# The router's small tables: from SBUF into a corner of the accumulator's PSUM bank

## Chip, cores and metric

One NeuronCore of a Trainium2 chip runs the whole program. The metric is the device time of one execution in microseconds (us). The profiled execution is one more run of the same program with the hardware profiler on.

## What is computed

Causal attention with a decaying bias, and behind it a layer of eight experts with one expert per token.

```
scores = q @ k.T / 8 ; bias = -(cum[i] - cum[j]),  cum = cumsum(max(s, 0))
attn   = softmax(where(causal, -1e9, scores + min(bias, 0)))      # 8 batches, 8 heads, 576 x 576
x      = (attn @ v) laid out as 4608 tokens x 512
logits = (x / |x|) @ (emb / |emb|).T / tau                        # 8 experts
e      = argmax(logits) ; gate = softmax(logits)[e]
out    = gate * (relu(x @ w1[e]) @ w2[e])                         # w1: 512 x 1024, w2: 1024 x 512
```

## The kernel before

The order of the work is written out by hand (`manual_schedule`): each engine runs its instructions in the order in which the Python code issues them, and the framework adds the semaphore waits that the data needs. For PSUM it orders any two accesses of different engines to the same bank, whether or not their columns overlap.

**Attention, 64 steps.** `step(n)` works on head `n`. In one step TensorE (PE) computes the scores of head `n` (`ta_`, `tb_`, `tbm`, `tbl`), a first pass of scores for head `n+5` from which VectorE (DVE) takes the row maxima (`s1`, `sa`, `s3`, `sb`; matmuls on L361, maxima on L369, L406 and L409), and at its end the product of probabilities and values of head `n-2` (`pv`, L525 to L527). Those products accumulate in columns 0 to 364 of one PSUM bank, the tile `om`. The score tiles `s` of the first pass have two buffers, so PE cannot start the third of a step before DVE has taken the maxima of an earlier one. ScalarE (ACT) does the exponentials (L497, L500) and casts. GpSimd (POOL) forms the low half of each probability, `PL = P - high half`, a subtraction with both inputs in SBUF (`pl_`, L251), 1024 and 576 columns per step, and issues the loads of q and k (L258, L338) and the scatters of finished tokens (L669). At the start of the next step DVE turns `om` into a finished head of tokens (`norm1` to `norm3`: L538, L542, L550). The heads of a batch are eight steps in a row.

**The router.** When the last head of batch `b` is normalised, `router(b, xt)` queues a chain of small DVE operations in `tasks`, and `slots` takes a few of them at the end of each step, up to the next `None`:

- first step: `sume` sums the logits (L79, 40 numbers per partition) and `sel1` takes their maxima (L607);
- second step: `sel2` marks the candidates (L611), `sel3` weighs them (L614);
- third step: `sel4` picks one (L618), `sel5` makes the one-hot table `oh` of it (L622);
- fourth step: PE ranks the tokens of each expert by ten small matmuls into columns 368 to 415 of `om` (`rank0`, L629 to L635), and at the end of that step DVE adds the base (L638, L640), selects (L646) and reduces to the target rows (L650).

The first batch's chain starts in step 10, and every eighth step after that. For batches 0 to 5 (`nb` is 8) it falls into the regular stretch of attention; batch 6 falls into the last steps, where the slots lie elsewhere, and batch 7 behind the loop. The scratch of the chain lies in SBUF, in slices of the tile `idx`: `IX["L"]` (40 columns: logits), `IX["T"]` (40: candidates, later ranks) and `IX["w"]` (5: maxima of the candidates). The columns of `IX["L"]` also serve once, in step 10, as a block of zeros that eight DMAs on the SP queue copy to the token table (`zr` in `setup4`, L241 and L242).

**The experts.** Behind step 63 the tokens are gathered by expert and run through both weight matrices (L891 and L967), the weights streaming in through a ring of buffers.

Of the kernel before, what the change touches and what calls it, by code (L numbers as in the profile page):

```python
# [76 lines left out]
def esum(nc, L, x):  # L77
    e = x.rearrange("p j (q a e) -> p j e q a", q=4, e=NE)[:, :, :, :, ::17]
    nc.vector.tensor_reduce(L, e, AX.XY, ALU.add)  # L79
# [35 lines left out]
def main(ctx, tc, qkh, qkc, vtin, s_in, emb, tau, w1h, w2h, out, shared, nb):  # L115
# [7 lines left out]
    ps_m, om = shared["ps_m"], shared["om"]  # L123
# [95 lines left out]
    IX = {}  # L219

    def setup4():
# [7 lines left out]
        nc.gpsimd.tensor_copy(IX["gp"], IX["tmp"].bitcast(I32))  # L229
        IX["L"], IX["T"], IX["w"] = t[:, 284:324], t[:, 324:364], t[:, 364:369]  # L230
        IX["r"], IX["E"] = t[:, 224:244], t[:, 244:284]
# [366 lines left out]
    def router(b, xt):  # L598
        R = {}

        def sume():
            R["L"] = IX["L"].rearrange("p (j e) -> p j e", j=5)
            esum(nc, R["L"], xt[:, :, 0:XW])

        def sel1():
# [1 line left out]
            nc.vector.tensor_reduce(m[:, 0], R["L"], AX.X, ALU.max)  # L607

        def sel2():
            T = R["T"] = IX["T"].rearrange("p (j e) -> p j e", j=5)  # L610
            nc.vector.tensor_tensor(T, R["L"], R["m"][:, 0].unsqueeze(2).to_broadcast([128, 5, NE]), op=ALU.is_ge)  # L611

        def sel3():
            nc.vector.tensor_tensor(R["T"], R["T"], wval, op=ALU.mult)  # L614

        def sel4():
            R["w"] = IX["w"]
            nc.vector.tensor_reduce(R["w"], R["T"], AX.X, ALU.max)  # L618

        def sel5():  # L620
# [16 lines left out]
        def rank1():  # L637
            nc.vector.tensor_tensor(R["T"], R["pr"][:, 0:40].rearrange("p (j e) -> p j e", j=5),  # L638
                                    base.unsqueeze(1).to_broadcast([128, 5, NE]), op=ALU.add)
            nc.vector.tensor_add(base, base, R["pr"][:, 40:40 + NE])  # L640
            if nb - 4 < b < nb - 1:
                nc.vector.tensor_copy(IX["cnt0"][:, 0:1], base[:, 0:1])
                nc.vector.tensor_scalar(base[:, 0:1], base[:, 0:1], float(SPL if b == nb - 3 else SPM), None, op0=ALU.max)

        def rank2():
            nc.vector.tensor_tensor(R["T"], R["T"], R["oh"], op=ALU.mult)  # L646

# [36 lines left out]

        sc = [P(scat, j) for j in range(5)]
        tasks.extend([sume, sel1, None, sel2, sel3, None, sel4, sel5, P(mq.append, rank)])

    X, WT, HT = {}, {}, {}
# [1010 lines left out]
```

## Time and profile before

| | |
|---|---|
| median of 3 runs | 828.55 us (827.26 to 832.63) |
| profiled execution | 827.8 us, of which 826.1 us span |
| PE busy | 769.1 us, 93% of the span |
| DVE, ACT, POOL busy | 556.5, 569.2 and 395.3 us |
| mean granted TensorE clock | 0.966 of full speed |
| regular attention (60 to 345 us) | PE busy 263.09 of 285.00 us, clock 0.96 |

PE's busy time is the time in which at least one matmul was in flight. The clock is the share of its upper level that the throttle granted. The profile names lines of the kernel (L622 is line 622), engines and tiles with buffer numbers left out.

### The profile page before, as it was taken

The page shows a single profiled execution, that of the slowest core. Times are in us where ns is not written, and L with a number is a line of the kernel's source. Part 1 is how long each engine was busy: PE and PEld are TensorE (multiplying, and loading weights), DVE is VectorE, ACT ScalarE, POOL GpSimd, SP SyncE. Part 2 cuts the span into 40 slices and gives each one's busy share as a digit, 9 for nine tenths or more (in the row PEclk, how much of TensorE's full clock was granted, in tenths as well). Part 3 has the DMA queues.
Part 4 walks back from the last instruction along what each step waited for, and adds up shares of the span by engine and source line. Part 5 has one row for each costly group of instructions (what it writes and reads, how often), then busy time and mean ns, then how long its engine had stood idle before and what let it go on. Part 6 is the DMA issues. An engine that isn't in the chain of part 4 may idle for free. (4 is left out here: it accounts for less than half of the span.)

```text
span 826.1 us, 20954 instructions
## 1 busy us (share of the span) xinstructions
PE 769.1 (93%) x7998; PEld 552.9 (67%) x7998; DVE 556.5 (67%) x1818; ACT 569.2 (69%) x1029; POOL 395.3 (48%) x375
## 2 busy tenths in 40 slices
PE   8998898989989898999789998989989989999997
PEld 4798897989989897988454554545444544554554
DVE  7787788787878888898557765654555556645621
ACT  9898688897969897887467865827637649376410
POOL 9997596887869796873432121220221112202001
PEclk9999899999989999999989999999999989999999
DMA  7798779595949797764534855643744746534001
GB/s 162 158 196 169 137 177 193 133 209 132 199 113 216 150 209 150 177 207 129 185 99 154 190 160 158 163 153 108 177 145 112 188 151 140 177 113 124 25 13 53
DMA packets 76002, 124.01 MB, mean 150 GB/s; under 512 B 38823, under 2 KB 39231, under 8 KB 75032
## 3 DMA queue, kind: packets, MB, share of 16 engines
q0 software_dynamic: 19632, 69.69, 36.2%
q1 hardware_dynamic: 56260, 52.84, 24.1%
q8 instruction: 71, 1.16, 0.6%
q14 instruction: 39, 0.32, 0.1%
HBM read 93.99 MB, written 21.49 MB: 140 GB/s over the span
## 5 line engine op out<-in xcount | busy, mean ns | idle before, releaser
L251 POOL TENSOR_TENSOR PL<-P 128x576 f16<-128x576 f32 (+2 forms) x128 | 205.1, 1709 | 31.9 <-ACT P L500 21.7
L891 PE MATMUL h<-xH,wt 128*128 128x512 f16 (+2 forms) x560 | 155.7, 360 | 0.8 <-DVE hq L922 0.3
L891 PEld LDWEIGHTS <-wt 128*128 128x128 f16 x960 | 86.8, 100 | 84.6 <-issue 11.9
L975 POOL DMA_INDIRECT out<-Kx,xj x39 | 44.1, 1130 | 195.2 <-DVE Kx L974 165.4
L361 PE MATMUL s<-qkb 96*128 96x288 f32 (+4 forms) x272 | 98.7, 377 | 22.4 <-DVE M L369 21.8
L525 PE MATMUL om<-vh,P 128*128 128x73 f16 x960 | 110.5, 201 | 3.0 <-DVE xt L550 2.3
L737 POOL DMA_INDIRECT Qx<-xs,idx x40 | 44.3, 1107 | 140.1 <-ACT vjunk L830 70.7
L526 PE MATMUL om<-vl,P 128*128 128x72 f16 x960 | 109.7, 199 | 0.0
L527 PE MATMUL om<-vh,PL 128*128 128x73 f16 x960 | 109.5, 200 | 0.0
L526 PEld LDWEIGHTS <-P 128*128 128x128 bf16 x960 | 96.5, 101 | 4.2 <-issue 3.6
L525 PEld LDWEIGHTS <-P 128*128 128x128 bf16 x960 | 95.7, 101 | 0.5 <-DVE xt L550 0.3
L527 PEld LDWEIGHTS <-PL 128*128 128x128 f16 x960 | 95.7, 100 | 0.0
L891 PE MATMUL h<-xL,wt 128*128 128x512 f16 (+1 forms) x264 | 94.9, 366 | 0.0
L967 PE MATMUL pxs<-wt,hq 128*128 128x512 f16 x360 | 90.3, 384 | 3.3 <-DVE wt L875 3.3
L500 ACT ACTIVATE P<-tb 128x1024 f32<-128x1024 f32 x64 | 65.1, 1018 | 24.8 <-PE tb L466 23.4
L369 DVE CUSTOM_DVE_ANT_0 junk<-s,mS 128x448 bf16<-128x448 f32 (+3 forms) x144 | 73.9, 520 | 5.3 <-PE s L361 3.2
L967 PE MATMUL pxs<-wt,hp 128*128 128x512 f16 x288 | 74.5, 387 | 0.0
L361 PEld LDWEIGHTS s<-qkb 96*128 96x128 f32 x272 | 51.9, 194 | 29.8 <-DVE M L369 27.9
L974 DVE TENSOR_SCALAR Kx<-pxs,xj,idx 128x512 f32<-128x512 f32 x39 | 31.5, 808 | 54.8 <-PE pxs L967 31.7
L967 PEld LDWEIGHTS <-hq 128*128 128x128 f16 x360 | 35.5, 99 | 46.5 <-ACT vjunk L749 3.6
L463 PE MATMUL tb<-QC,KC 128*128 128x448 f32 (+3 forms) x256 | 64.5, 310 | 0.0
L459 PE MATMUL tb<-qkb 128*128 128x448 f32 (+3 forms) x256 | 62.0, 289 | 0.0
(309 smaller groups left out, 1962.1 us busy)
## 6 DMA issues: line engine op xcount, KB each, us to landing
qkb<-qkh POOLq DMA_DIRECT2D x15, 1216.0 KB
ring<-w2h SPq DMA_DIRECT2D x44, 256.0 KB
ring<-w1h SPq DMA_DIRECT2D x36, 256.0 KB
KC<-qkh POOLq DMA_DIRECT2D x14, 576.0 KB
QC<-qkh POOLq DMA_DIRECT2D x14, 576.0 KB
vT<-vtin SPq DMA_DIRECT2D x24, 320.0 KB
rw<-w1h SPq DMA_DIRECT2D x15, 256.0 KB
rw<-w2h SPq DMA_DIRECT2D x12, 256.0 KB
```

What stands on the lines that cost most here:

```text
L251: nc.gpsimd.tensor_tensor(out, a, b_, op=ALU.subtract)
L361: nc.tensor.matmul(out, G[g]["QB"][0:96, h, 128 * i:128 * i + 128], G[g]["KB"][0:96, h, lo:hi], start=True, stop=True)
L369: nc.vector.tensor_tensor_reduce(out=jk, in0=src, in1=ms, scale=1.0, scalar=NEG, op0=ALU.add, op1=ALU.max, accum_out=MP[n // 2][:, n % 2, ...
L459: nc.tensor.matmul(out, G[g]["KB"][:, h, ks:ks + 128], G[g]["QB"][:, h, 64 + qlo:64 + qhi], start=start, stop=False)
L463: nc.tensor.matmul(out, HD[n]["KC"][:, ks:ks + 128], HD[n]["QC"][:, qlo:qhi], start=False, stop=stop)
L500: nc.scalar.activation(HD[n]["P32"][:, 576:1600], HD[n]["tb"], AF.Exp, scale=0.125)
L525: nc.tensor.matmul(out, lh, vh[:, kb], start=(kb == 0), stop=False)
L526: nc.tensor.matmul(out[:, u:u + 72], lh, vl[:, kb], start=False, stop=False)
L527: nc.tensor.matmul(out, ll, vh[:, kb], start=False, stop=(kb == j))
L737: ins = nc.gpsimd.indirect_dma_start(out=x.bitcast(I32), out_offset=None, in_=src, in_offset=bass.IndirectOffsetOnAxis(ap=X[("i", e, t)][1 ...
L891: nc.tensor.matmul(h, w[:, 128 * c:128 * c + 128], x[:, c, lo:hi], start=(c == 0 and k == 0), stop=(c == 3 and k == 2))
L967: nc.tensor.matmul(y, h, w, start=(m == 0 and k == 0), stop=(m == 7 and k == 2))
```

## The change

For batches 0 to 5 the three scratch areas of the router become columns 416 to 500 of the PSUM bank `om`: logits 416 to 455, candidates 456 to 495, maxima 496 to 500. For batches 6 and 7 they stay in `idx`. Nothing else is edited.

```diff
         def sume():
-            R["L"] = IX["L"].rearrange("p (j e) -> p j e", j=5)
+            R["L"] = (IX["L"] if b > nb - 3 else om[:, 416:456]).rearrange("p (j e) -> p j e", j=5)
             esum(nc, R["L"], xt[:, :, 0:XW])
...
-            T = R["T"] = IX["T"].rearrange("p (j e) -> p j e", j=5)
+            T = R["T"] = (IX["T"] if b > nb - 3 else om[:, 456:496]).rearrange("p (j e) -> p j e", j=5)
...
-            R["w"] = IX["w"]
+            R["w"] = IX["w"] if b > nb - 3 else om[:, 496:501]
```

No instruction is added, taken away or moved on any engine; operands and waits of DVE's instructions change. In DVE's list, at the end of the router's third step of the first batch (`vl` is the low half of the values, `rm` the row maxima of the logits, `wsel` a constant table in SBUF, `oh` the one-hot table, `z` the first operation of the next step's normalisation; names in brackets are the engines or DMA queues whose semaphores are waited for):

```order
 L310 SCALAR_TENSOR_TENSOR vl<-V,sc,vh_109 128x3x144 [waits Activation_49]
-L618 TENSOR_REDUCE idx<-idx 128x5
-L622 TENSOR_TENSOR oh<-wsel,idx 128x40 [waits DVE_49]
-L538 TENSOR_SCALAR z<-om 128x5 [waits PE_49]
+L618 TENSOR_REDUCE om<-om 128x5 [waits PE_49]
+L622 TENSOR_TENSOR oh<-wsel,om 128x40 [waits DVE_49]
+L538 TENSOR_SCALAR z<-om 128x5
 L369 ISA junk,M<-s_1623,mS 128x448 [waits PE_49]
```

L622 keeps its place; one of its two tensor inputs is now in PSUM. The wait for PE's accumulation, which stood at L538, stands two instructions earlier.

In DVE's list, at the ends of the first and of the second step of the first batch's router:

```order
 L310 SCALAR_TENSOR_TENSOR vl<-V,sc,vh_109 128x3x144 [waits Activation_49]
-L79 TENSOR_REDUCE idx<-xt 128x40 [waits DMAHW4_49,DMAHW3_49,DMAHW5_49,DMAHW2_49,DMAHW6_49,DMAHW1_49,DMAHW7_49,DMAHW0_49,Pool_49]
-L607 TENSOR_REDUCE rm<-idx 128x5 [waits DVE_49]
-L538 TENSOR_SCALAR z<-om 128x5 [waits PE_49]
+L79 TENSOR_REDUCE om<-xt 128x40 [waits PE_49]
+L607 TENSOR_REDUCE rm<-om 128x5 [waits DVE_49]
+L538 TENSOR_SCALAR z<-om 128x5
```

```order
-L611 TENSOR_TENSOR idx<-idx,rm 128x40
-L614 TENSOR_TENSOR idx<-idx,wval 128x40 [waits DVE_49,Pool_49]
-L538 TENSOR_SCALAR z<-om 128x5 [waits PE_49]
+L611 TENSOR_TENSOR om<-om,rm 128x40 [waits PE_49]
+L614 TENSOR_TENSOR om<-om,wval 128x40 [waits DVE_49,Pool_49]
+L538 TENSOR_SCALAR z<-om 128x5 [waits DVE_49]
```

At L79 the waits for the eight DMAs and for POOL go, in this batch alone (the other batches' L79 had none), and a wait for PE comes; at L611 a wait for PE comes two instructions ahead of where it stood.

## Rows read from the trace of the kernel before

**Rows 1.** The page's first part: busy us, share of the span, instructions by engine.

```profile
PE 769.1 (93%) x7998; PEld 552.9 (67%) x7998; DVE 556.5 (67%) x1818; ACT 569.2 (69%) x1029; POOL 395.3 (48%) x375
```

**Rows 2.** Waits, PE, 60 to 350 us: total us, times, longest us.

```profile
PE s L361 <- DVE M L369: 21.5, 9, 3.4
```

**Rows 3.** DVE in order of time around 137 us: start us, us, engine, line.

```profile
136.78 0.18 DVE L618 TENSOR_REDUCE idx<-idx 128x5 f32<-128x40 f32 x1
137.00 4.08 DVE L622 TENSOR_TENSOR oh<-wsel,idx 128x40 bf16<-128x40 f32 x1
141.01 0.15 DVE L538 TENSOR_SCALAR z<-om 128x5 f32<-128x5 f32 x1
```

**Rows 4.** POOL in the same stretch and the one behind it.

```profile
135.52 3.36 POOL L251 TENSOR_TENSOR PL<-P 128x576 f16<-128x576 f32 x2
...
139.12 1.90 POOL L251 TENSOR_TENSOR PL<-P 128x576 f16<-128x576 f32 x1
143.89 1.90 POOL L251 TENSOR_TENSOR PL<-P 128x1024 f16<-128x1024 f32 x1 [2.88 <-ACT P L500]
```

**Rows 5.** PE in the same stretch; in brackets the idle time before, and its releaser.

```profile
136.51 0.20 PE L527 MATMUL om<-vh,PL 128*128 128x73 f16 x1
...
141.75 0.40 PE L361 MATMUL s<-qkb 96*128 96x288 f32 x1 [3.33 <-DVE M L369]
...
146.78 0.20 PE L527 MATMUL om<-vh,PL 128*128 128x73 f16 x1
```

**Rows 6.** Single steps between ends of accumulation: length; PE, PEld, DVE, ACT, POOL; clock; DMA.

```profile
78.27:85.24 6.97, 5.07 (x73) 4.70 (x73) 4.67 (x20) 5.05 (x8) 4.73 (x4) 1.00 0.42 109
171.54:176.63 5.09, 5.07 (x73) 4.70 (x73) 4.64 (x20) 5.06 (x8) 4.03 (x4) 1.00 0.64 188
90.22:101.78 11.56, 8.24 (x83) 7.77 (x83) 8.07 (x19) 6.17 (x10) 6.17 (x5) 0.70 0.74 130
136.71:146.98 10.27, 6.94 (x83) 6.51 (x83) 8.10 (x19) 6.22 (x10) 6.20 (x5) 0.83 0.78 145
181.55:191.78 10.23, 6.89 (x84) 6.47 (x83) 8.11 (x19) 6.24 (x10) 6.21 (x5) 0.83 0.80 149
226.33:237.95 11.62, 8.26 (x83) 7.78 (x82) 8.13 (x19) 6.24 (x10) 6.23 (x5) 0.72 0.71 134
272.70:280.27 7.57, 5.39 (x83) 5.02 (x83) 6.77 (x19) 5.58 (x9) 6.64 (x5) 1.00 1.05 183
314.89:325.12 10.23, 6.91 (x83) 6.48 (x83) 8.06 (x19) 6.23 (x10) 6.20 (x5) 0.83 0.82 148
```

**Rows 7.** Single lines: times, ns min/median/max, first and last start, forms.

```profile
L622 DVE TENSOR_TENSOR oh<-wsel,idx x8: 194/4064/4104, 90.5 to 386.9; 128x40 bf16<-128x40 f32 x8
L611 DVE TENSOR_TENSOR idx<-idx,rm x8: 190/730/742, 85.2 to 385.4; 128x40 f32<-128x40 f32 x8
L550 DVE TENSOR_TENSOR xt<-om,z x64: 531/533/535, 37.5 to 381.5; 128x360 f32<-128x360 f32 x64
L310 DVE SCALAR_TENSOR_TENSOR vl<-V,sc,vh x63: 496/646/668, 31.6 to 375.9; 128x432 f16<-128x432 f32 x32, 128x288 f16<-128x288 f32 x31
L638 DVE TENSOR_TENSOR idx<-om,base x8: 189/200/201, 101.8 to 391.7; 128x40 f32<-128x40 f32 x8
L646 DVE TENSOR_TENSOR idx<-idx,oh x8: 189/192/194, 102.1 to 392.9; 128x40 f32<-128x40 f32 x8
L640 DVE TENSOR_TENSOR base<-base,om x8: 161/162/164, 102.0 to 391.9; 128x8 f32<-128x8 f32 x8
```

**Rows 8.** The SP queue in step 10.

```profile
78.73 0.22 SPq L242 DMA_DIRECT2D xs<-idx  x1
```

**Rows 9.** DVE's first router instruction in the first and in the third batch.

```profile
80.25 0.73 DVE L79 TENSOR_REDUCE idx<-xt 128x40 f32<-128x320 f32 x1 [1.84 <-POOL PL L251]
...
171.61 0.77 DVE L79 TENSOR_REDUCE idx<-xt 128x40 f32<-128x320 f32 x1
```

**Rows 10.** Eight steps of batch 4, columns as in rows 6.

```profile
257.77:299.96 42.19, 39.99 (x586) 38.92 (x586) 35.74 (x141) 37.04 (x49) 35.33 (x31) 1.00 0.85 178
```

## The prediction

> **What bounds the kernel now.** I read the page's first part first: PE is busy in 93% of the span [rows 1], so the end moves only if PE's idle time or its clock changes. Next I asked whom PE waits for in the regular attention steps. One line carries nearly all of it: 21.5 us in 9 waits, the longest 3.4 us, of the first-pass score matmul for DVE's maxima [rows 2]. Nine waits in some fifty steps are not a steady bound but accidents, so I looked for what DVE does just before one. In the third router step of batch 1, L622, an operation on 40 numbers per partition, lasts 4.08 us [rows 3]. The same instruction takes 194 ns at its shortest, its median is 4064 ns [rows 7]. Its normalisation (L538) starts only when it ends, the maxima behind that, and PE's matmul at 141.75 has then idled for 3.33 us [rows 3, 5].
>
> What holds L622? POOL subtracts in that stretch, with both inputs in SBUF, and L622 has both inputs in SBUF too. L622 ends at 141.08 by its row, and POOL's last subtraction at 141.02 [rows 3, 4]. That subtraction of 576 columns took 1.90 us, as long as the next one of 1024 columns that ran alone [rows 4], so the two engines hinder each other. L611, also with two SBUF inputs, swings between 190 and 742 ns [rows 7]. Operations that take one tensor from PSUM and one from SBUF don't swing, though they run beside POOL's subtractions in every step: L550 takes 531 to 535 ns in 64 steps, and L310, which has two sizes, never more than 668 ns [rows 7]. So the hold belongs to the pair of SBUF inputs.
>
> The price to PE is more than the idle time. A window from one end of accumulation to the next shows a whole step (the borders are ends of L527, as 136.71 and 146.98) [rows 5]. The six steps with a held L622 last 11.56, 10.27, 10.23, 11.62, 7.57 and 10.23 us. [...] In batch 4 the hold was shorter, PE idled 2.18 us, and the clock stayed at 1.00 [rows 6]. [...]
>
> **The change part by part.**
>
> *The hold of L622.* In the changed kernel one of its inputs is in PSUM for batches 0 to 5. Its price then is that of its shortest run, 0.19 us, in place of 4.08. What would a step without the hold last? Batch 4 tells: 7.57 less 2.18 idle is 5.39 us, at full clock, with the ten ranking matmuls in it, and PE busy 5.39 [rows 6]. Six steps together now last 61.48 us; six of 5.39 are 32.34. The difference is **29.1 us**. By kind: six idle times (3.32, 3.33, 3.34, 3.36, 2.18, 3.32) make 18.9 us, and 10.3 us are lost clock.
>
> *The wait at L79 in batch 0.* It starts at 80.25 us after 1.84 us of idle time. The profile names POOL, but the order shows waits for eight DMAs as well, and the last of these is issued by SP at 78.73 [rows 8, 9]; it copies zeros out of the columns that L79 overwrites. With the logits in PSUM this wait is gone. PE idled for 1.90 us in that step, which was 6.97 us long with PE busy for 5.07; the same step of batch 2 took 5.09 [rows 6]. That is **1.9 us**. POOL's constants, which L614 still needs, are wanted one step later; I cost them at nothing: POOL works them off ahead of the subtractions of the same step, and PE needs those.
>
> *The hold of L611.* It falls from 0.73 to about 0.2 us in six steps, 3 us of DVE time. DVE's slack hides it: of the 21.5 us in nine waits [rows 2], the six held steps take 18.9 and batch 0's L79 takes 1.90 (above), which leaves 0.75 us in two waits for everything else. So 0, and 0.75 us for the low end.
>
> *PSUM in place of SBUF for seven small operations a batch.* The nearest rows with PSUM and SBUF inputs at the same size are L638 and L646: median 200 and 192 ns, the 8 ns times 42 instructions is 0.3 us, off the path in most places: 0. No row shows DVE writing PSUM. Its bound from above: if each of the six writing instructions of a batch cost a whole further short operation (0.2 us), 36 times that is 7 us of DVE time, of which DVE's slack takes most; from below, nothing speaks for a gain. I take 0.
> [...]
>
> *The new waits for PE.* L79, L611 and L618 now wait for PE's accumulation, which before was waited for at L538. Queued behind them on DVE is the next step's normalisation, and it waited for the same matmuls. L618 started at 136.78, and PE's accumulation had ended at 136.71; L79 of batch 2 at 171.61, against 171.54 [rows 3, 5, 6, 9]. So they stand behind the end already: 0, with up to 0.1 us each (18 of them, 2 us) for the high end. PE's own list of instructions and awaited semaphores is unchanged.
>
> *What is late next.* Once L622 is quick, DVE has 4.2 us of work left in the held step (8.10 less 3.9) [rows 6], in 5.39 us. Over eight steps, 42.19 us with 2.18 idle in batch 4, ACT was busy 37.04, POOL 35.33 and DMA 0.85 of the time [rows 10]. In 40.0 us that is 93%, 88% and 0.90: tight, but under one, and these engines work one to two steps ahead of PE. So PE stays the bound. If they were not ahead enough, the cost is bounded by the second rival below.
>
> Sum: 29.1 + 1.9 = 31.0 us. The profiled execution took 827.8 us, so 796.8; the median of the runs lies 0.75 us above that execution, which gives **797.5 us**. The experts' stage starts 31 us earlier and is otherwise the same, as its loads are issued by the step that attention has reached.
>
> **The rivals.**
>
> *1. The hold stays.* What is in PSUM is L622's second input; the first, the constant table, stays in SBUF. L550, L310 and L638 have PSUM first. The only row with SBUF first and PSUM second is L640, steady at 161 to 164 ns [rows 7], but POOL was not subtracting at that point, so it proves little. If the order of the inputs matters, only the 1.9 us of batch 0 are saved: 826.7. For it: no row tests it. Against it: both orders need one SBUF stream and one PSUM stream.
> [...]
>
> *2. The idle time goes, but the rest does not follow.* ACT, POOL or DMA, which caught up during each hold (ACT worked 6.2 us in the held steps and 5.58 in batch 4's), no longer can, and PE meets small waits for them, or the granted clock falls at other places. Only the idle times are won: 18.9 + 1.9 = 20.8, or 807.7 us. For it: ACT at 93%. Against it: batch 4, whose eight steps ran at clock 1.00 with one third less idle time in the held one, and whose PE was busy for 39.99 of the 40.0 us that remain [rows 10].
>
> *3. Slower.* Router and accumulator now share a bank, and each of the 18 new waits at L79, L611 and L618 could hold DVE until the semaphore of PE's last matmul is seen, with the whole of the next maxima behind it. It decides the sign only where a wait costs more than 31.0/18 = 1.7 us, about the length of a whole accumulation; at 2.3 us each the time would be 827.8 + 41.4 - 31.0 + 0.75, some 839. Against it: the 0.07 us above.
>
> **How the numbers follow.** Forecast 0.78, rival 1 0.07, rival 2 0.12, rival 3 0.03. The forecast's own spread: 0.75 us less for L611, 1.3 us less by the fastest of the runs shown, and window borders that are good to about 0.2 us in each of seven steps, so 794; upward 2 us for waits and up to 7 for the writes to PSUM. Rival 2 reaches to 808. The range 793 to 808 leaves out rivals 1 and 3 and the tails, about 2 in 10. About 1% (8 us) is what a measurement of this kernel tells from no change. Faster by over 1%: forecast and rival 2, 0.90. Within 1%: rival 1, 0.07. Slower: rival 3, 0.03.
>
> **What would show it.** In the changed kernel L622 should read about 0.2 us in batches 0 to 5 (and as before in the last two), L611 too. PE's wait for the maxima should fall from 21.5 us to under 2, the six steps to about 5.4 us, the clock in them to 1.00, and L79 in batch 0 should start at about 78.4. If L622 is still some 4 us long, rival 1 is right. If it is short but steps last longer than 5.4 us, with PE waiting for ACT, POOL or a DMA, rival 2. If L79, L611 and L618 show idle time before them and PE waits behind, rival 3. I would be most wrong if the held time was only hiding a lag of POOL, which then appears as PE waiting for its low halves.

## The result and the profile after

The changed kernel takes 791.47 us (median of 4 executions, 788.12 to 793.67). The kernel before, beside it, takes 827.90 us (4 executions, 826.80 to 832.63). The ratio is 0.956, with an interval of 0.950 to 0.963. The profiled execution of the changed kernel is the slowest of its four, 793.67 us; against the profiled one of before (827.8) it gains 34.1 us, where 31.0 were predicted.

The page's first part, the same columns as [rows 1]:

```profile
span 792.0 us, 20951 instructions
...
PE 756.0 (95%) x7998; PEld 543.4 (69%) x7998; DVE 532.0 (67%) x1818; ACT 567.5 (72%) x1029; POOL 393.1 (50%) x375
```

PE works 13.1 us less than before on the same 7998 matmuls; its mean granted clock is 0.982 instead of 0.966, so more of them ran at the higher level, and its share of the span rises from 93% to 95%. DVE works 24.5 us less on the same number of instructions.

Waits of PE, 60 to 350 us, as in [rows 2] (total us, times, longest us):

```profile
PE om L525 <- DVE xt L550: 2.3, 2, 2.0
PE s L361 <- DVE M L369: 0.6, 2, 0.4
```

The score matmul's wait for the maxima fell from 21.5 us in 9 waits to 0.6 us in 2. One wait of 2.0 us, for L550, is in this stretch now; the kernel before has one of the same length at its own end of attention, behind 350 us. The last section comes back to it.

Single lines, as in [rows 7] (times, ns min/median/max, first and last start, shape). Those on `om` are batches 0 to 5, those on `idx` the last two:

```profile
L622 DVE TENSOR_TENSOR oh<-wsel,om x6: 195/195/196, 88.5 to 287.9; 128x40 bf16<-128x40 f32 x6
L611 DVE TENSOR_TENSOR om<-om,rm x6: 184/208/208, 83.3 to 282.8; 128x40 f32<-128x40 f32 x6
L638 DVE TENSOR_TENSOR om<-om,base x6: 207/208/208, 93.3 to 292.8; 128x40 f32<-128x40 f32 x6
L638 DVE TENSOR_TENSOR idx<-om,base x2: 188/188/189, 329.5 to 359.4; 128x40 f32<-128x40 f32 x2
```

L622 is down from a median of 4064 ns to 195, within 1 ns in all six batches. L611 no longer swings. L638 stands in both forms, but its two late runs are faster in either kernel: in batches 0 to 5 it took 199 to 201 ns before, so writing to PSUM instead of SBUF costs it 8 ns.

The held step of batch 1 again, DVE and then POOL in order of time, as in [rows 3] and [rows 4]:

```profile
128.06 0.20 DVE L618 TENSOR_REDUCE om<-om 128x5 f32<-128x40 f32 x1
128.30 0.20 DVE L622 TENSOR_TENSOR oh<-wsel,om 128x40 bf16<-128x40 f32 x1
128.41 0.16 DVE L538 TENSOR_SCALAR z<-om 128x5 f32<-128x5 f32 x1
```

```profile
126.81 3.36 POOL L251 TENSOR_TENSOR PL<-P 128x576 f16<-128x576 f32 x2
129.75 1.39 POOL L338 DMA_DIRECT2D QC<-qkh  x1
130.41 1.90 POOL L251 TENSOR_TENSOR PL<-P 128x576 f16<-128x576 f32 x1
```

L622 starts at 128.30, in the middle of POOL's subtractions as before, and is done in 0.20 us. (A row with x2 holds one subtraction of 576 and one of 1024 columns; it prints the shape of the first.) POOL's next subtraction of 576 columns takes 1.90 us, exactly as long as the one in [rows 4], though L622 is not held now.

The six steps, the step with L79 of batch 0, and the eight steps of batch 4, with the columns of [rows 6] (length; busy time of PE, PEld, DVE, ACT, POOL with instruction counts; clock; DMA share; GB/s):

```profile
88.17:93.29 5.12, 5.12 (x83) 5.05 (x83) 4.06 (x19) 5.05 (x8) 5.12 (x5) 1.00 1.12 203
127.99:133.12 5.13, 5.13 (x83) 5.06 (x83) 4.06 (x19) 5.05 (x8) 5.13 (x5) 1.00 1.08 202
...
78.14:83.24 5.10, 5.06 (x74) 4.70 (x73) 4.64 (x19) 5.05 (x8) 4.67 (x4) 1.00 0.48 130
...
237.10:277.61 40.51, 39.99 (x586) 39.02 (x586) 32.84 (x141) 36.91 (x49) 35.07 (x30) 1.00 0.88 185
```

The other four steps read 5.12 each, so the six last 30.73 us instead of 61.48. PE is busy for the whole of each, at clock 1.00. The step with L79 in batch 0 went from 6.97 to 5.10.

The whole span in two stages of each kernel, attention from the same point on and then the experts, first before and then after:

```profile
78.27:381.00 302.73, 277.74 (x3953) 268.77 (x3953) 249.85 (x912) 247.29 (x341) 230.82 (x191) 0.96 0.75 171
381.00:826.10 445.10, 418.14 (x3262) 223.31 (x3258) 244.56 (x655) 251.16 (x601) 92.87 (x87) 0.96 0.47 131
```

```profile
78.14:348.70 270.56, 265.84 (x3954) 258.92 (x3953) 225.69 (x912) 245.90 (x341) 230.24 (x191) 1.00 0.83 191
348.70:792.00 443.30, 417.02 (x3261) 223.79 (x3258) 244.21 (x655) 250.90 (x601) 91.36 (x87) 0.97 0.47 132
```

Of the 34.1 us, attention gives 32.2 (302.73 less 270.56) and the experts' stage 1.8 (445.10 less 443.30). Attention's 32.2 is made of 30.75 in the six steps and 1.87 at L79, less 0.45 us for slightly longer steps elsewhere.

### The profile page after: what moved, and what is told of

The parts are those of the page before. It is cut to its first block, busy times and chain, and to the rows that moved or that the text cites. A ratio compares the mean times of both kernels' runs of the same rounds, so it can differ in the third digit from the quotient of the medians.

```text
span 792.0 us, 20951 instructions
## 1 busy us (share of the span) xinstructions
PE 756.0 (95%) x7998; PEld 543.4 (69%) x7998; DVE 532.0 (67%) x1818; ACT 567.5 (72%) x1029; POOL 393.1 (50%) x375
## 5 line engine op out<-in xcount | busy, mean ns | idle before, releaser
L525 PE MATMUL om<-vh,P 128*128 128x73 f16 x960 | 106.9, 199 | 3.0 <-DVE xt L550 2.3
L526 PE MATMUL om<-vl,P 128*128 128x72 f16 x960 | 106.4, 196 | 0.4 <-issue 0.4
L527 PE MATMUL om<-vh,PL 128*128 128x73 f16 x960 | 106.2, 198 | 0.1
L361 PE MATMUL s<-qkb 96*128 96x288 f32 (+4 forms) x272 | 96.3, 368 | 1.6 <-DVE M L369 0.9
L526 PEld LDWEIGHTS <-P 128*128 128x128 bf16 x960 | 94.7, 99 | 4.5 <-issue 4.1
L525 PEld LDWEIGHTS <-P 128*128 128x128 bf16 x960 | 93.8, 99 | 0.5 <-DVE xt L550 0.3
L527 PEld LDWEIGHTS <-PL 128*128 128x128 f16 x960 | 93.9, 98 | 0.2 <-issue 0.2
L867 ACT ACTIVATE wt<-ring,idx 128x512 f16<-128x512 f32 x80 | 53.7, 711 | 10.0 <-DVE idx L857 7.8
```

Of the source, the lines that this page charges most:

```text
L361: nc.tensor.matmul(out, G[g]["QB"][0:96, h, 128 * i:128 * i + 128], G[g]["KB"][0:96, h, lo:hi], start=True, stop=True)
L525: nc.tensor.matmul(out, lh, vh[:, kb], start=(kb == 0), stop=False)
L526: nc.tensor.matmul(out[:, u:u + 72], lh, vl[:, kb], start=False, stop=False)
L527: nc.tensor.matmul(out, ll, vh[:, kb], start=False, stop=(kb == j))
L867: nc.scalar.activation(h, a, AF.Copy, scale=s)
```

## The experiments

The theory, called H in the expectations: DVE's L622, with two SBUF inputs, is held while POOL reads SBUF; that lateness alone is the price. Its rivals: the hold slows POOL too, and that is part of the price; the gain comes from the other tiles that moved; or the clock would have fallen without the idle time. (POOL's subtraction reads and writes SBUF; no run here separates the two, and none moves or removes the subtractions. That they are what holds L622 rests on the ends of the rows: in five of the six batches it ends 0.06 or 0.07 us behind the end of a subtraction, in batch 4 0.27 us. In batch 7, with no subtraction beside it, it takes 0.19 us.) Where an experiment's end of attention is given, it is the end of the last accumulation there: 381.00 us in the kernel before, 348.70 in the changed one.

**One part of the change alone: the maxima.** Only the second input of L622 moves to PSUM; logits and candidates stay in SBUF.

```
 def sel4():
-    R["w"] = IX["w"]
+    R["w"] = IX["w"] if b > nb - 3 else om[:, 496:501]
```

> Part of the change alone: only the maxima of the candidates (the input of L622) move to PSUM for batches 0 to 5; logits and candidates stay in SBUF. Theory H (the gain is L622, which no longer has two SBUF inputs and so is not held while POOL subtracts): L622 about 0.2 us in the six batches, PE's wait for the maxima falls by some 19 us, L611 stays at 0.73 us, L79 of batch 0 waits for the DMAs again (1.9 us): 793 to 796 us. Rival B (the gain comes from the other operands, or from the waits that moved): above 815 us.

Measured: 796.11 us (791.97 to 798.65), ratio 0.964 with an interval of 0.958 to 0.970, against 825.79 beside it: at the upper end of what was expected for H. Two of its single lines and the step with L79:

```profile
L622 DVE TENSOR_TENSOR oh<-wsel,om x6: 195/195/196, 90.0 to 291.4; 128x40 bf16<-128x40 f32 x6
...
L646 DVE TENSOR_TENSOR idx<-idx,oh x8: 189/727/1527, 95.2 to 365.2; 128x40 f32<-128x40 f32 x8
```

```profile
78.06:84.77 6.71, 5.06 (x73) 4.70 (x73) 4.67 (x20) 5.04 (x8) 4.72 (x4) 1.00 0.36 102
```

Five columns per partition carry most of the gain: attention ends at 353.4, which is 27.6 of the 32.3 us. L79's wait is back (6.71 instead of 5.10). New is L646. Before it was steady at 189 to 194 ns [rows 7]; now it runs earlier beside POOL's subtractions (in all six of batches 0 to 5), and with two SBUF inputs it takes up to 1.53 us, ending each time 0.06 or 0.07 us behind a subtraction. Removing one hold uncovered the next, and moving the logits as well takes that one away too.

**The other part alone: logits and candidates.** The changed kernel with L622's inputs back in SBUF.

```
 def sel4():
-    R["w"] = IX["w"] if b > nb - 3 else om[:, 496:501]
+    R["w"] = IX["w"]
```

> The rest of the change alone: logits and candidates in PSUM, the maxima of the candidates in SBUF, so L622 has two SBUF inputs again. Theory H: L622 about 4.06 us again, six steps of 10 to 11.6 us, clock in them 0.7 to 0.83; L611 at 0.21 and the wait at L79 gone: 824 to 829 us. Rival B: below 805 us.

Measured: 818.46 us (811.47 to 820.88), ratio 0.989 with an interval of 0.982 to 0.997. The line, and its first and fifth held step:

```profile
L622 DVE TENSOR_TENSOR oh<-wsel,idx x8: 193/4066/4127, 88.4 to 384.9; 128x40 bf16<-128x40 f32 x8
```

```profile
88.13:98.38 10.25, 6.89 (x83) 6.47 (x83) 8.11 (x19) 6.23 (x10) 6.21 (x5) 0.83 0.84 148
...
269.03:278.15 9.12, 6.94 (x83) 6.51 (x83) 6.94 (x19) 6.11 (x10) 6.97 (x5) 0.81 0.99 167
```

L622 is held as before, and the six steps last 61.85 us. Attention ends at 379.0, 2.0 us earlier than before; the step with L79 alone went from 6.97 to 5.11 us. The total fell by more than that and below the 824 to 829 us expected: in the profiles the experts' stage took 438.9 us here and 445.1 before, and that stage scatters (below). L611 is free here (185 to 208 ns) and that gained nothing: the six steps it stands in last 4.92 or 4.93 us here and 4.91 to 4.97 before, so its term of 0 was right.

**DVE late by a set time, with the change in place.** Memsets of a scratch tile behind L622, which read nothing, make DVE late. The same edit with three lists of columns; (1024, 880) and (1024,) * 6 replace the list in the other two. This adds work that the reference doesn't have.

```
 def sel5():
...
     nc.vector.tensor_tensor(oh, ...)
+    if b < nb - 2:
+        for n in (1024, 1024, 1024, 384):
+            nc.vector.memset(junk[:, 0:n], 0.0)
```

> The changed kernel, with DVE kept busy for about 3.9 us behind L622 in batches 0 to 5 by memsets that read nothing (extra work that the result doesn't need). Theory H, with the price on PE as the prediction has it (DVE's lateness alone: idle time and then clock): PE idles 3.3 us in six steps and the clock of these steps falls to 0.7 to 0.83: 29 us over the changed kernel, 817 to 824 us. Rival C (part of the loss was POOL's, slowed by the shared use): under 815 us.

> As the run before, with about 2.1 us of memsets. If the clock falls only after the longer idle times, as batch 4 of the kernel before suggests (2.18 us of idle time, clock 1.00): PE idles about 1.5 us in six steps, clock 1.00 in them, 9 us over the changed kernel: 799 to 803 us. If every idle time costs clock as well: 808 us or more.

> The changed kernel with about 3.9 us of memsets behind L622 in batches 0 to 5 (extra work that the result doesn't need); the two runs before reached only 2.1 and 1.1 us. Theory H with the loss all from DVE's lateness: PE idles 3.3 us and the clock falls in all six steps, 5.2 to 6.5 us each: 820 to 827 us. Rival C (POOL's slowing was part of the loss): below 815 us.

The longer of the first two gave 802.81 us (800.73 to 806.24; ratio 0.974, 0.967 to 0.980) and the short one 796.29 us (795.19 to 797.88; 0.965, 0.960 to 0.971), both below what was expected. The memsets were half as long as planned: 1024 columns of bf16 ran as 512 of uint32 in 485 ns, and L538 started 2.3 and 1.2 us behind the start of L622. Hence the third, with six of them: 3.9 us, where the hold had made it 4.0 (2.85 in batch 4). The memsets of the third, then steps of the first (two), the second and the third (two):

```profile
L626 DVE MEMSET junk<- 128x512 uint32 x36 | 17.5, 485 | 5.5 <-DVE junk L626 5.2
```

```profile
88.08:96.61 8.53, 6.94 (x83) 6.52 (x83) 5.83 (x23) 6.10 (x10) 6.22 (x5) 0.80 0.99 177
131.20:138.18 6.98, 5.40 (x83) 5.02 (x83) 5.67 (x23) 5.60 (x9) 5.87 (x5) 1.00 1.08 205
```

```profile
88.33:94.47 6.14, 5.38 (x83) 5.01 (x83) 5.01 (x21) 5.59 (x9) 5.87 (x5) 1.00 1.09 195
```

```profile
88.25:98.64 10.39, 6.92 (x83) 6.50 (x83) 7.17 (x25) 6.10 (x10) 6.22 (x5) 0.84 0.81 146
223.18:234.90 11.72, 8.26 (x83) 7.79 (x82) 7.17 (x25) 6.24 (x10) 6.22 (x5) 0.71 0.71 132
```

With 3.9 us the time is 825.02 us (821.32 to 828.12, 10 executions) against 824.08 beside it, ratio 1.001 with an interval of 0.999 to 1.004: the whole gain is gone, though L622 itself takes 195 to 197 ns. PE waits 21.2 us in 7 waits for the maxima (21.5 in 9 before), and attention ends at 381.0 as before. Five of the steps last 10.36 to 10.45 us at clock 0.84, one 11.72 at 0.71, close to the two sizes of the held steps in [rows 6]. That the totals meet is in part chance: the 1.9 us at L79 stay won, and batch 4's step lasts 10.44 instead of 7.57, as the delay is the same in all six batches. The sizes of the steps are what counts: DVE's lateness alone makes the price. That the hold slows POOL as well is not needed for any of it, and that rival falls.

The lengths also show what a step is made of. In the short one PE idles 6.14 − 5.38 = 0.76 us, and the step is 1.02 longer than the clean 5.12. In the longer one it is 6.98 − 5.40 = 1.58 of idle time, and 1.86 more than 5.12. PE's busy time itself is 0.26 to 0.28 us higher where the step was interrupted, at clock 1.00, and the trace shows where that lies. Around the interrupted matmul, first in the clean step and then in the one with the short delay:

```profile
89.35 0.51 PE L463 MATMUL tb<-QC,KC 128*128 128x448 f32 x2
89.70 0.29 PE L361 MATMUL s<-qkb 96*128 96x288 f32 x1
```

```profile
89.51 0.51 PE L463 MATMUL tb<-QC,KC 128*128 128x448 f32 x2
90.78 0.40 PE L361 MATMUL s<-qkb 96*128 96x288 f32 x1 [0.76 <-DVE M L369]
```

In the clean step L361 starts 0.16 us before the matmul ahead of it ends, and the two overlap; behind a wait there is nothing to overlap with, and L361 itself takes 0.11 us more. That restart is paid once: 0.26 us behind 0.76 of idle time, 0.28 behind 1.58.

**The changed kernel once more**, with more executions.

> The changed kernel once more, beside the next three, to size its gain and its spread: 788 to 794 us; attention (to the end of its last accumulation) within 1 us of the first profile, differences between executions in the experts' stage.

Measured: 790.22 us (786.42 to 793.97, 6 executions) against 824.08 (23 executions), ratio 0.959 with an interval of 0.955 to 0.963: 33.9 us. Its two stages:

```profile
0.00:349.85 349.85, 339.22 (x4740) 319.65 (x4741) 288.02 (x1163) 316.81 (x428) 301.77 (x288) 1.00 0.84 187
349.85:788.80 438.95, 414.43 (x3260) 222.06 (x3258) 244.66 (x655) 251.04 (x601) 92.02 (x87) 0.98 0.47 133
```

The experts' stage of the same program took 443.30 us in one execution and 438.95 in the other; attention was 1.2 us longer in the second, where within 1 was expected.

**Which property of L622 is held?** In the kernel before, L622 is split into five operations of 8 columns, each with one SBUF tensor and, as its scalar, a pointer to one of the maxima, all in SBUF.

```
 def sel5():
...
+    if b < nb - 2:
+        for j in range(5):
+            nc.vector.tensor_scalar(oh[:, j, :], wsel, R["w"][:, j:j + 1], None, op0=ALU.is_equal)
+        return
...
```

> The kernel before, all scratch in SBUF, but L622 of batches 0 to 5 split into five operations of 8 columns that take the constant table as their one tensor and a maximum as a per-partition number. Theory H in its narrow form (two SBUF tensors): each operation 0.1 to 0.2 us, no hold of 4 us, PE's idle time in these steps under 0.5 us; L611 and L646 may be held, as in the run with the maxima alone in PSUM; L79 waits as before: 794 to 801 us. Rival D (anything that DVE reads and writes in SBUF alone is held, PSUM itself is the cure): operations of up to 4 us and 820 us or more.

Measured: 829.56 us (824.16 to 832.35, 10 executions), ratio 1.007 with an interval of 1.004 to 1.010. The line, then DVE and POOL around the first of them:

```profile
L624 DVE TENSOR_SCALAR oh<-wsel,idx x30: 218/219/4071, 91.7 to 327.3; 128x8 bf16<-128x8 f32 x30
```

```profile
91.43 0.18 DVE L618 TENSOR_REDUCE idx<-idx 128x5 f32<-128x40 f32 x1
91.65 4.51 DVE L624 TENSOR_SCALAR oh<-wsel,idx 128x8 bf16<-128x8 f32 x5
96.08 0.15 DVE L538 TENSOR_SCALAR z<-om 128x5 f32<-128x5 f32 x1
```

```profile
90.10 3.35 POOL L251 TENSOR_TENSOR PL<-P 128x576 f16<-128x576 f32 x2
93.05 1.37 POOL L338 DMA_DIRECT2D QC<-qkh  x1
93.71 1.88 POOL L251 TENSOR_TENSOR PL<-P 128x576 f16<-128x576 f32 x1
```

The five take 4.46 to 5.09 us together in every one of the six batches. So the narrow form of the theory, that only two SBUF tensors are held, falls: an operation with one SBUF tensor is held as well. Open was whether its scalar, read from SBUF, counts as the second input. The last experiment moves only that to PSUM (the same split, with `R["w"]` in `om[:, 496:501]` for batches 0 to 5).

> The five operations with a per-partition number of the run before, but with the maxima in PSUM, so that the number is read from PSUM and the constant table, the one tensor, from SBUF. Theory H2 (the second SBUF read of that operation was the per-partition number): no hold, 795 to 802 us. Theory H3 (the operation with one SBUF tensor and an SBUF result is held by itself, whatever its number is read from): the first of five held for 4.07 us again, 824 to 832 us.

Measured: 831.18 us (824.28 to 832.03, 10 executions) against 823.44, ratio 1.009 with an interval of 1.005 to 1.013.

```profile
L624 DVE TENSOR_SCALAR oh<-wsel,om x30: 223/224/4062, 91.1 to 326.1; 128x8 bf16<-128x8 f32 x30
```

Still held, up to 4.06 us. It is not where the scalar lies, then; this form of operation, from one SBUF tensor to SBUF, is held by itself. So a pair of SBUF inputs is what holds the two-tensor form of L622, but it is not a condition for every hold. It isn't every operation with one SBUF input: L618, a reduction from SBUF to SBUF in the same stretch, takes 0.18 us [rows 3]. Why that form is held, no run shows.

**All eight batches in PSUM.** The conditions `b > nb - 3` become `b > nb`, so the last two batches move as well.

> The change extended to batches 6 and 7. Their held time was small (L622 0.50 and 0.19 us), so theory H gives at most 1 us: 788 to 794 us, as the changed kernel. If the shared bank's new waits matter where DVE and PE meet at the end of attention (batch 7's chain runs between the experts' first matmuls), 2 to 5 us more.

Measured: 788.66 us (788.04 to 793.88, 6 executions), ratio 0.959 with an interval of 0.956 to 0.962, against 0.959 (0.955 to 0.963) of the changed kernel on the same chip: no difference. L622 reads 189 to 197 ns in all eight batches, and attention ends at 348.7 as in the first profile of the changed kernel. The last two batches were losing little there: in the changed kernel their L622 takes 192 and 496 ns. No run was faster than the changed kernel beyond the noise.

## Why the prediction was right in kind and short in size

- **The hold of L622** belongs to its SBUF inputs, as predicted: 195 ns six times, and 4.07 us again as soon as only its own inputs go back (the second experiment). As a general cause the pair of SBUF inputs does not stand (L624, with one). One reading behind it was too broad: of the 64 runs of L550 only 28 lie mainly beside a subtraction, of L310 54; they are as steady there as elsewhere (L550 531 to 534 ns beside one, 531 to 535 elsewhere; L310 at most 668 and 664). Also right is that PE pays twice, for idle time and for clock: the delay of 3.9 us alone brings back 21.2 us of waits and clocks of 0.71 to 0.84. What the clock does inside a held step shows in the trace of before, behind the wait of batch 1 that ends at 141.75: windows of half a microsecond read 1.00 up to 142.5, 0.50 from 143.0 to 146.0 and 1.00 again from 146.5, and the matmuls of L525 to L527 start about 62 ns apart at 0.50 and 34 ns apart at 1.00.
- **The step that was off: "Batch 4 tells: 7.57 less 2.18 idle is 5.39 us".** A step without a hold lasts 5.12 us. Batch 4's step had been through an idle time, and taking the idle time off leaves the restart in: about 0.27 us of busy time, the same behind 0.76, 1.58 and 2.18 us. Six times 0.27 is the 1.6 us that the term of 29.1 lacked; it measured 30.75. A better base was in the trace of before: its steps without any wait and without the ten ranking matmuls mostly last 4.80 to 5.02 us, and those ten started 25 ns apart, which adds 0.25.
- **The rest of the miss is the total, not the change.** The forecast was 6.0 us above the median: 3.1 because the profile pair gained 34.1 instead of 31.0 (1.6 from the term above, 1.8 from the experts' stage, less 0.3 in small terms), 0.75 for setting the median above the profiled execution, and 2.2 because the profiled execution of the changed kernel lies that much above its median. The last two are the chance of which execution was profiled. The experts' stage was said to be "otherwise the same". In its instructions it is, but it lasts 437.8 to 445.1 us over the profiles of all these kernels, and the kernel before was seen in the longest of them. The low end took in 1.3 us by three executions; ten of the changed kernel spread over 786.4 to 794.0.
- **L79 in batch 0**: 1.9 predicted, 1.87 measured (6.97 to 5.10), and back to 6.71 where the logits stay in SBUF. Right.
- **L611 and the PSUM operations at 0**: right. L611 freed alone gains nothing. Operations on PSUM cost 4 to 14 ns more each in batches 0 to 5 (L607 201 for 197, L638 208 for 200, L618 196 for 184, L646 207 for 193), far below the bound of 200 ns, and DVE has the slack: it is busy for 4.06 us of the 5.12 of a step in which L622 ran.
- **New waits at 0**: right. L618 starts at 128.06 with the accumulation ended at 127.99, 0.07 us as before, and L79 at 78.21 behind 78.14. So the rival "slower" falls.
- **The rival "hold stays"** falls: an operation with SBUF first and PSUM second, beside POOL's subtractions, takes 195 ns. L640, which lies beside them now in batches 0 to 5, takes 161 to 164 as before.
- **The rival "the rest does not follow"** falls: the eight steps last 40.51 us with PE busy 39.99, at clock 1.00. ACT is at 91%, POOL at 87%, and no wait for either appears among PE's waits.
- **"The two engines hinder each other" was wrong in one direction.** POOL's 576 columns take 1.90 us with a quick L622 too; only DVE is held. The trace of before shows another reason for the 1.90. Alone, 576 columns take 1.15 us, and the long record begins while POOL's own load of q is being issued:

```profile
128.32 1.15 POOL L251 TENSOR_TENSOR PL<-P 128x576 f16<-128x576 f32 x1 [0.85 <-ACT P L497]
...
138.46 1.38 POOL L338 DMA_DIRECT2D QC<-qkh  x1
```

The end of that issue, 139.84, and 1.15 us more give 140.99; the subtraction of [rows 4] ends at 141.02.

## What to carry to other kernels

L622, on 40 columns, swung from 194 to 4104 ns here, and that was a hold, not work. Where an operation swings like that, look at what GpSimd reads from SBUF in that stretch, and try one of the operation's inputs in PSUM. That freed the form with two tensors (4064 to 195 ns); the form with a tensor and a scalar stayed held with its scalar in PSUM (up to 4062 ns). In a kernel bound by PE, price the hold by the lateness of the matmul that waits at the end of it, with the clock behind the idle time (0.70 to 0.84 here) and a restart (0.27 us here), and take the clean step from a step that never idled. Before trusting a difference of a few us in the total, compare one stage: here the end of attention told 2 us where the totals of equal work scattered by 7.

## What the runs showed of the hardware that was not expected

- A held DVE operation can miss the gap between two subtractions of POOL. In the split version five operations of 0.22 us start at 91.65; POOL's pair ends at 93.45, its next begins at 93.71, and DVE is through only at 96.16, after that one's end at 95.59. In the kernel before L622 sat through such a gap in five of the six batches (4.06 to 4.10 us), where a subtraction of 1024 columns that ran alone took 1.90. In batch 4 it did not: POOL's pair ended at 275.64 and the next subtraction began at 275.85, a gap of 0.21 us; L622 ended at 275.91, while that next one ran on to 277.79.

```profile
272.99 2.92 DVE L622 TENSOR_TENSOR oh<-wsel,idx 128x40 bf16<-128x40 f32 x1
```

```profile
272.25 3.39 POOL L251 TENSOR_TENSOR PL<-P 128x576 f16<-128x576 f32 x2
275.19 1.43 POOL L338 DMA_DIRECT2D QC<-qkh  x1
275.85 1.94 POOL L251 TENSOR_TENSOR PL<-P 128x576 f16<-128x576 f32 x1
```

  The issue of a load (L338) lies across the gap in all of these cases, so it does not tell them apart. In batch 4 L622 started 0.8 us before the first subtraction of the pair ended, in the other five at most 0.04 us. What decides is not shown.
- Eight columns in the tensor_scalar form are held as long as 40 in the two-tensor form (4071 ns at most, and a median of 4064).
- PE's clock did not answer to idle time alone. Behind 0.76 us of it the granted clock fell in 0 of 6 steps, behind 1.58 in 2 of 6 with the same instructions, behind 2.18 in one of two (batch 4: 1.00 before, 0.81 in the second experiment), behind 3.3 to 4.4 in all 28 seen (0.70 to 0.84 over the five of the kernel before and the six with the delay of 3.9 us). Behind the wait at L79, 1.65 to 2.05 us long, it fell in one of four (the first split version, 0.81). A fall cost about 1.55 us (8.53 against 6.98), or nearly twice that: the step of 11.62 us, less 3.36 idle and 5.39, leaves 2.87.
- What looks like the same hold is left at another place, in both kernels. In the changed one, DVE and POOL near 336 us:

```profile
335.38 3.87 DVE L875 SCALAR_TENSOR_TENSOR wt<-rw,idx,wt 128x512 f16<-128x512 f32 x1
...
340.61 0.74 DVE L875 SCALAR_TENSOR_TENSOR wt<-rw,idx,wt 128x512 f16<-128x512 f32 x1
```

```profile
335.67 3.02 POOL L251 TENSOR_TENSOR PL<-P 128x576 f16<-128x576 f32 x2
```

L875 takes 0.74 us at 340.61 and 3.87 us beside POOL's pair, and L550 behind it makes PE idle for 1.97 us: the 2.0 us wait shown above. In the kernel before L875 takes 3.87 us at 367.70, with the same wait. Moving one input of L875 was not tried.
